# Two transformer layers on one core: other score blocks at the end of layer 1, whole score groups repeated, a later stop of the VectorE units

## The chip, the cores and the metric

The kernel runs on one core of one Trainium2 chip. The metric is the device time in microseconds (us); the time before is the median of seven runs. A separate run was profiled; its trace gives every instruction of every engine, the DMAs, and the clock that was granted to TensorE.

## The reference

Two layers of attention and a feed-forward part, with the same weights twice. Sequence 2048, width 448, 16 heads of 28, hidden width 1792, all in bf16.

```python
def _A_ref(x, wqkv, wo):
    B, S, D = x.shape
    H = 16; Dh = D // H
    qkv = (x @ wqkv).reshape(B, S, 3, H, Dh).transpose(2, 0, 3, 1, 4)
    q, k, v = qkv[0], qkv[1], qkv[2]
    scores = jnp.einsum("bhqd,bhkd->bhqk", q, k) * Dh ** -0.5
    p = _softmax(scores, axis=-1)
    o = jnp.einsum("bhqk,bhkd->bhqd", p, v)
    return o.transpose(0, 2, 1, 3).reshape(B, S, D) @ wo

def _B_ref(x, w1, b1, w2, b2):
    h = jnp.einsum("bsd,df->bsf", x, w1) + b1
    r = jnp.where(h > 0, h, 0)
    return jnp.einsum("bsf,fd->bsd", r * r, w2) + b2

for _ in range(2):
    x = x + _A_ref(_layernorm(x), A_wqkv, A_wo)
    x = x + _B_ref(_layernorm(x), B_w1, B_b1, B_w2, B_b2)
```

## The kernel before

**Who orders the work.** The kernel is written as a set of streams (Python generators) that yield operations with an engine, a planned duration, dependencies and a buffer to take. A planner (`Planner.run`) keeps a planned clock for each engine and always takes the stream whose next operation can start first, with priorities in between; the order in which it takes them is the order in which the instructions stand on the engines' queues. So a change of one number can move instructions everywhere behind the place where it first matters.

**Blocks, passes and units.** The rows (queries) of each layer are cut into blocks, listed in `blocks` (L228) as (first tile of 128 rows, tiles). A pass is one block and one group of four heads. A unit is 512 columns of scores of one head: two key tiles for a block of 256 rows (r = 2), four for one of 128 (r = 4). Each layer has 1024 units, however it is cut.

**Scores and exps.** `s_stream` (L693) takes three units at a time into one PSUM tile `sc` of 1536 columns; there are two such tiles. Its matmuls (L739) have 32 rows, one head each, so the three of one round (one value of `i`) work side by side in different quarters of the array. `e_stream` (L748) turns a group into probabilities `pt` with one exp of 1536 columns on ScalarE (L757). A group can be computed only when the exp two groups earlier has released its `sc` tile, and has to be ready when the exp just before it is over.

**Repeats.** TensorE's planned load over the last `HWIN` = 3.4 us is kept near `HOT` = 0.9 (`HOTE` = 0.8 for the last 100 units). Where it is lower, `s_stream` writes some of the group's matmuls again ahead of the group itself, up to `MORE` = 3 times; the results are the same values in the same places. The number is bounded by the planned room: until another operation could start on TensorE, and until the exp before is over. Each repeat counts 0.22 us in the plan. The loop over rounds is

```python
o.more = 0.22 * again
for i in [0] * again + list(range(4)):
    for k, (pi, kb, r, hh) in enumerate(us):
        if i >= r:
            continue
```

so a repeat is the first round of the group. A second filler, `heat` (L1079), puts matmuls of 448 columns on an identity (L1094) where the load is under `HEAT`.

**Units on VectorE.** `apart` (L661) sometimes gives a fourth unit to the group; its scores go into another PSUM bank (`mt`), and VectorE computes its exp with integer and polynomial steps (`a_first`, `a_rest`, L780 to L825), seven instructions. None is taken when fewer than `STOP` = 140 units remain.

**What follows.** `p_stream` (L830) multiplies probabilities by values into `oT` (L885); the denominators come along as a row of ones in the values. `norm_stream` (L942) divides: by a way over three small DMAs on SP's queue (`dn`, `scr`, `rec`), or, for the last block of a layer, by a matmul with `sel` (L957) and a reciprocal. `chain` (L1009) then adds the output projection to `x_sb`, normalises (`layernorm`, L422; the transposed tile is copied out of PSUM at L472 or L474), computes the hidden layer (L523, relu L1042 or L1044, square L1048), the second matrix, and adds or stores. `engs_now()` allows ScalarE as well as VectorE for a copy once no scores are left.

Of the kernel before, what the change touches and what calls it, by code (L numbers as in the profile page):

```python
# [11 lines left out]
DT = mybir.dt  # L12
AF = mybir.ActivationFunctionType
ALU = mybir.AluOpType
P = 128
H = 16
DH = 28
DHP = 32
G = 4
QB = 512  # L20
QR = 256
# [11 lines left out]
TILES = 1  # L33
DCLK = 0.2
OWN = 2
TG = 1
SUMS = 0
HALF = 320
BB = 0.85
TURNS = 1  # L40
# [30 lines left out]
LASTP = 3.2  # L71
# [1 line left out]
HOLD1 = 7  # L73
NL = 0
NLP = 3.8
STOP = 140
HSTOP = 0
CHUNK = 2
EV = 3.5
# [124 lines left out]
def kernel(  # L204
# [12 lines left out]
    nc = tc.nc  # L217
# [7 lines left out]

    q_scale = float(DH) ** -0.5 * float(np.log2(np.e)) * 2.0 ** 23

    blocks = [[(0, 2), (2, 2), (4, 2), (6, 2), (8, 2), (10, 2), (12, 2), (14, 2)], [(0, 2), (2, 2), (4, 2), (6, 2), (8, 2), (10, 2), (12, 1), (13, 1), (14, 1), (15, 1)]]  # L228

    x_view = A_x[0].rearrange("(tb p) d -> p tb d", p=P)  # L230
    out_view = out[0].rearrange("(tb p) d -> p tb d", p=P)
# [15 lines left out]
    pl = Planner()  # L247
# [131 lines left out]
    def bank(o, name):  # L379

        if o.res in R_m:
            return ps_m[R_m.index(o.res)].tile([P, 512], DT.float32, name=name, tag="m")[:, :]
        return ps_sc.tile([P, 3 * 512], DT.float32, name="sc", tag="sc")[:, 0:512]
# [18 lines left out]
    def engs_now(early=False):  # L402
        return ("ACT", "DVE") if (early and ("s", AEND) not in pl.tok) or len(s_left) == 0 else ("DVE",)
# [18 lines left out]
    def layernorm(t0, nt, deps_of, early=False, mv=None):  # L422


        if mv is None:
            mv = moments()
            for j in range(nt):
                yield stats(mv, t0, j, deps_of(j))
        ln = {}
        single = early and t0 == 0 and TILES  # L430
        rss = []
        for a, b in [(0, 1), (1, 2)] if single else [(0, nt)]:
            def rsqrt(e, a=a, b=b):
                rstd = sp.tile([P, 4], DT.float32, name="rstd")
                for j in range(a, b):
                    ln[j] = rstd[:, j:j + 1]
                ve = sp.tile([P, 4], DT.float32, name="ve")
                nc.gpsimd.tensor_tensor(out=ve[:, a:b], in0=mv[0][:, a:b, 1], in1=eps_t[:, a:b], op=ALU.add)  # L438
                nc.gpsimd.tensor_tensor(out=rstd[:, a:b], in0=ve[:, a:b], in1=mhalf[:, a:b], op=ALU.pow)  # L439
            rs = Op("POOL", 0.95 if early else 0.6, rsqrt, deps=[mv[1][b - 1]], sets=[("rs", t0 + a)] if early else ())  # L440
            rss += [rs] * (b - a)
            pl.spawn(EV, iter([rs]))
        box = {}

        def take(e):
            box["x"] = xtp.tile([P, NDC, QR], DT.bfloat16, name="xnT")
        own_xt = Op("DVE", 0.0, take, acq=R_xt)
        yield own_xt
        xnT = box["x"]
        ends = []  # L450
        todo = []
        evs = []

        def turn(p0, own, xs):
            box = {}

            def tr(e, xs=xs):
                tp = bank(t, "tp").bitcast(DT.bfloat16).rearrange("p (c q) -> p c q", c=NDC)
                box["t"] = tp
                for k, (xn, _) in enumerate(xs):  # L460
                    for dc in range(NDC):
                        nc.tensor.transpose(out=tp[:, dc, k * P:(k + 1) * P],  # L462
                                            in_=xn[:, dc * P:(dc + 1) * P], identity=ident[:, :])
            t = Op("PE", 0.07 * NDC * len(xs), tr, deps=[x[1] for x in xs],
                   acq=pools_now(early) if early else spare(1))
            yield t

            def ev(e, p0=p0, w=len(xs) * P):
                tp = box["t"]
                dst = xnT[:, :, p0 * P:p0 * P + w]  # L470
                if e == "ACT":
                    nc.scalar.copy(out=dst, in_=tp[:, :, 0:w])  # L472
                else:
                    nc.vector.tensor_copy(out=dst, in_=tp[:, :, 0:w])  # L474
            o = Op("DVE" if early else engs_now(), 0.12 + 0.3 * len(xs), ev, deps=[t], rel=t, sets=[("xT", t0 + p0)] if early else ())
            ends.append(o)
            evs.extend([o, Op("DVE", 0.0, None, deps=[t], rel=own)])

        wide = 1 if single else 2
        for p0 in range(0, nt, wide):  # L480
            js = range(p0, min(p0 + wide, nt))
            own = Op("DVE", 0.0, None, acq=R_xn)
            yield own
            xs = []
            for j in js:
                xn = xns[2 * (own.turn % 2) + j % 2]

                def norm(e, j=j, xn=xn):
                    nc.vector.tensor_scalar(out=xn[:, 0:D], in0=x_sb[:, t0 + j, :],  # L489
                                            scalar1=mv[0][:, j, 0:1], scalar2=ln[j],  # L490
                                            op0=ALU.subtract, op1=ALU.mult)
                nm = Op("DVE", 0.42, norm, deps=[rss[j]], sets=[("n", t0, j)] if early else ())
                yield nm
                xs.append((xn, nm))

            todo.append((p0, own, xs))
            if early and p0 + wide < nt:
                continue
            while todo:
                p0, own, xs = todo.pop(0)  # L500
                yield from turn(p0, own, xs)
        yield from evs
        return xnT, own_xt, ends
# [148 lines left out]
    gbuf = []  # L652
    where = {}
# [39 lines left out]
    def s_stream():  # L693
        while at[0] < len(units):
# [5 lines left out]
            def fn(e, gi=gi, us=us, js=js):  # L700
# [28 lines left out]
                    last = ("e" in gbuf[gi - 1] and gbuf[gi - 1]["e"].end) or pl.clock["ACT"] + 1.35  # L729
                    again = max(0, min(MORE, int(min(o.room, last - LAT["PE"] - o.end) / 0.22)))  # L730
                o.more = 0.22 * again
                for i in [0] * again + list(range(4)):
                    for k, (pi, kb, r, hh) in enumerate(us):
                        if i >= r:
                            continue
# [94 lines left out]
    def p_stream():  # L830


        for pi, (l, qb, g, kbs, first, last) in enumerate(passes):
# [15 lines left out]
                yield Op("-", 0.0, None, deps=[("u", pi, kb)])  # L849
                yield Op("-", 0.0, None, deps=[("e", gi) for gi, k, _ in where[pi, kb] if k < 3])  # L850
            yield from got(hold)
            if end and SUMS:
                box["so"] = Op("PE", 0.0, None, acq=pools_now)
                yield box["so"]
            while todo:
                now = [kb for kb in todo if done(kb)][:some]
                if len(now) < min(some, len(todo)):
# [11 lines left out]
                todo = [kb for kb in todo if kb not in now]  # L869
                begin, close = "t" not in box, not todo  # L870

                def fn(e, now=now, begin=begin, close=close, box=box, pi=pi, l=l, g=g, r=r, n=n, end=end):
                    if "t" not in box:
                        p_next[0] = None
                        box["t"] = bank(box["o"], "oT")
                        if "so" in box:
                            box["s"] = bank(box["so"], "den")
                    held[0] -= sum(k == 3 for kb in now for _, k, _ in where[pi, kb])
                    for kb in now:
                        for i in range(r):  # L880
                            for gi, k, hh in where[pi, kb]:
                                p, c0 = gbuf[gi]["pt"], k * 512 + i * n
                                if k == 3:
# [4 lines left out]
                                                 start=begin and kb == now[0] and i == 0,  # L888
                                                 stop=close and kb == now[-1] and i == r - 1,
                                                 tile_position=(0, DHP * hh))  # L890

                            for gi, k, hh in where[pi, kb] if end and SUMS else ():
                                p, c0 = (gbuf[gi]["pd"], i * n) if k == 3 else (gbuf[gi]["pt"], k * 512 + i * n)
                                nc.tensor.matmul(box["s"][DHP * hh:DHP * hh + DHP, 0:n],
                                                 lhsT=ones[:, :], rhs=p[:, c0:c0 + n],
                                                 start=begin and kb == now[0] and i == 0,
                                                 stop=close and kb == now[-1] and i == r - 1,
                                                 tile_position=(0, DHP * hh))
                by = [(("x" if k == 3 else "e"), gi) for kb in now for gi, k, _ in where[pi, kb]]
                o = Op("PE", 0.02 + 0.22 * len(now) * (2 if end and SUMS else 1), fn,  # L900
                       deps=[*by, *{("V", l, kb + i) for kb in now for i in range(r)}],
                       acq=None if "o" in box else pools_now(),
                       rel=[gbuf[gi][w] for w, gi in by], mode="col")
                box.setdefault("o", o)
                yield o
            res = {}
            if end and SUMS:
                pl.spawn(2, last_norm(l, qb, g, n, box, o))
                return

            def ev(e, box=box, first=first, last=last, g=g, res=res, n=n, l=l, qb=qb):
                src = box["t"][:, 0:n]
                if last:
# [10 lines left out]
            if last:  # L924
                pl.spawn(3, norm_stream(l, qb, g, res, oe))

    def last_norm(l, qb, g, n, box, o):
        def rcp(e):
            box["r"] = rp.tile([P, QR], DT.float32, name="rec")
            nc.vector.reciprocal(out=box["r"][:, 0:n], in_=box["s"][:, 0:n])  # L930
        r = Op("DVE", n * 0.0066 + 0.1, rcp, deps=[o], rel=box["so"], acq=R_rec)
        yield r

        def mul(e):
            nc.vector.tensor_tensor(out=oTn_of[l, qb][0][:, g, 0:n], in0=box["t"][:, 0:n], in1=box["r"][:, 0:n], op=ALU.mult)
        m = Op("DVE", 0.15 + n / 930, mul, deps=[r, oTn_of[l, qb][1]], rel=[box["o"], r])
        yield m
        norm_done.setdefault((l, qb), []).append(m)
        if len(norm_done[l, qb]) == G:
            pl.spawn(LASTP, chain(l, qb))  # L940

    def norm_stream(l, qb, g, res, oe):  # L942


        t0, nt = blocks[l][qb]
        n = nt * P
        box = {}
        tail = qb == len(blocks[l]) - 1 and not (l == 1 and SUMS and g < G - TG)
        if (l, qb) not in oTn_of:
            def take(e):  # L950
                oTn_of[l, qb][0] = np_.tile([P, G, QR], DT.bfloat16, name="oTn")
# [191 lines left out]
```

## Time and profile before

| | us |
|---|---|
| median of 7 runs | 925.67 |
| lowest and highest | 922.99, 926.24 |
| profiled execution | 932.32 |
| its span, first to last instruction | 930.5 |
| its granted TensorE clock (mean) | 0.974 |
| first exp begins, last one ends | 10.96, 913.55 |

In the page's rows the numbers after the bar are busy time, mean duration of one, and the idle time of the engine just before such instructions, with what ended it. The durations of one exp overlap (1642 ns each, but 888.8 us for 659). In the timeline a row merges equal instructions that follow each other: start, length, what, count, and the idle time ahead in brackets. In the windows each row is one stretch of time: its length, the busy time (and count) of each engine, then the granted clock as a share of full speed.

### The profile page before, as it was taken

The numbers are of one execution on the slowest core, as the hardware profiler recorded it, in microseconds if no ns is written. First come the engines' busy times: TensorE is split into PE (matmuls) and PEld (weight loads), VectorE is DVE, ScalarE is ACT, GpSimd is POOL, SyncE is SP. The second block draws the span as 40 slices with busy tenths as digits, with TensorE's granted clock in tenths as the row PEclk, the third lists the DMA queues.
The fourth block names the chain that finished last, engine by engine and source line by source line (L and its number), as shares of the span: only waits on it lengthen the run. The fifth ranks groups of instructions, "written<-read, shape, count | busy, mean of one in ns | idle before, by whom it ended". The sixth has DMA issues, their size and how long they took to land.

```text
span 930.5 us, 30373 instructions
## 1 busy us (share of the span) xinstructions
PE 825.4 (89%) x13553; PEld 474.9 (51%) x13553; DVE 665.7 (72%) x1387; ACT 899.4 (97%) x679; POOL 40.5 (4%) x91
## 2 busy tenths in 40 slices
PE   8999879988889898888989999889989988898888
PEld 4555545454455544554545454545454444555556
DVE  7754778778887877787867564678687788867444
ACT  6999999999999999999999999999999999999994
POOL 5100000000000000000000000000000000000000
PEclk9999989999999999999999999979899999989999
DMA  7100010000000000000000000011000000010000
GB/s 230 59 2 2 8 38 14 15 10 13 13 14 8 14 14 8 14 14 1 2 1 2 2 2 1 9 39 31 21 11 23 24 14 19 14 25 12 22 18 12
DMA packets 34624, 18.53 MB, mean 20 GB/s; under 512 B 18618, under 2 KB 34043, under 8 KB 34492
## 3 DMA queue, kind: packets, MB, share of 16 engines
q1 hardware_dynamic: 34492, 16.58, 6.3%
q8 instruction: 106, 1.74, 0.8%
q14 instruction: 26, 0.21, 0.1%
HBM read 14.26 MB, written 2.07 MB: 18 GB/s over the span
## 4 chain that ended last, share of the span: by engine, by line
ACT 64%; PE 17%; issue 16%; DVE 2%; POOL 0%; DMA 0%; ACTq 0%; DVEq 0%
ACT pt L757 64%; PE mt L523 6%; PE sc L739 5%; PE oT L885 3%; PE sc L523 1%; PE mt L1094 0%; DVE xn L489 0%; PE tp L462 0%; DMA x_sb<-in_A_x_dram 0%; DVE vh L809 0%; POOL rstd L439 0%; DVE st L416 0%; DVE x_sb L1006 0%; DVE xnT L474 0%; PE mt L739 0%
## 5 line engine op out<-in xcount | busy, mean ns | idle before, releaser
L757 ACT ACTIVATE pt<-sc 128x1536 bf16<-128x1536 f32 x659 | 888.8, 1642 | 12.3 <-PE sc L739 10.2
L739 PE MATMUL sc<-Q_sb,K_sb 32*128 32x256 bf16 (+1 forms) x6094 | 328.6, 266 | 95.9 <-ACT pt L757 90.5
L739 PEld LDWEIGHTS <-K_sb 32*128 32x128 bf16 x6324 | 166.4, 93 | 261.5 <-issue 250.2
L885 PE MATMUL oT<-pt,V_sb 128*32 128x256 bf16 (+1 forms) x4456 | 158.2, 272 | 0.2
L885 PEld LDWEIGHTS <-V_sb 128*32 128x32 bf16 x4608 | 97.6, 99 | 46.9 <-issue 41.3
L523 PE MATMUL mt<-xnT,w 128*128 128x256 bf16 (+1 forms) x960 | 117.4, 264 | 0.6 <-DVE r L1044 0.2
L809 DVE SCALAR_TENSOR_TENSOR vh<-vh,vm 128x512 f32<-128x512 f32 x142 | 97.2, 685 | 1.7
L523 PEld LDWEIGHTS <-w 128*128 128x128 bf16 x1008 | 81.0, 98 | 31.2 <-issue 21.5
L1044 DVE TENSOR_SCALAR r<-mt 128x512 bf16<-128x512 f32 (+1 forms) x107 | 72.7, 679 | 31.5 <-PE mt L523 30.6
L786 DVE TENSOR_SCALAR vi<-mt 128x512 int32<-128x512 f32 x71 | 48.9, 688 | 31.5 <-PE mt L739 26.3
L1006 DVE TENSOR_TENSOR x_sb<-x_sb,mt 128x448 bf16<-128x448 bf16 (+1 forms) x62 | 37.6, 607 | 36.8 <-PE mt L523 36.6
L523 PE MATMUL mt<-w,h 128*128 128x448 bf16 x224 | 52.8, 355 | 0.0
L919 DVE COPY oT_sb<-oT 128x256 f32<-128x256 f32 (+1 forms) x52 | 19.9, 382 | 43.6 <-PE oT L885 43.5
L809 DVE SCALAR_TENSOR_TENSOR vh<-vm 128x512 f32<-128x512 f32 x71 | 48.3, 680 | 0.0
L523 PE MATMUL mt<-w,V_sb 128*128 128x448 bf16 (+1 forms) x210 | 47.9, 353 | 0.0
L438 POOL TENSOR_TENSOR ve<-mv,eps_t 128x2 f32<-128x2 f32 (+1 forms) x35 | 8.4, 241 | 876.0 <-DVE mv L417 852.5
L416 DVE BATCH_NORM_STATS2 st<-x_sb 128x6 f32<-128x448 bf16 x64 | 39.4, 616 | 1.2 <-DMA x_sb<-in_A_x_dram 0.6
L739 PE MATMUL mt<-Q_sb,K_sb 32*128 32x256 bf16 (+1 forms) x230 | 39.4, 273 | 0.0
L545 DVE CAST K_sb<-mt 128x512 bf16<-128x512 f32 (+1 forms) x30 | 20.4, 680 | 22.2 <-PE mt L523 22.1
L523 PE MATMUL mt<-xnT,wk 128*128 128x256 bf16 x240 | 33.4, 279 | 0.6 <-DVE K_sb L919 0.4
L489 DVE TENSOR_SCALAR xn<-x_sb,mv,rstd 128x448 bf16<-128x448 bf16 x64 | 26.0, 420 | 10.7 <-POOL rstd L439 9.4
L523 PE MATMUL mt<-xnT,wq 128*128 128x256 bf16 x248 | 33.5, 274 | 0.0
(90 smaller groups left out, 658.8 us busy)
## 6 DMA issues: line engine op xcount, KB each, us to landing
rec<-scr SPq DMA_DIRECT2D x52, 128.0 KB
x_sb<-in_A_x_dram SPq DMA_DIRECT2D x8, 224.0 KB
out_dram<-x_sb SPq DMA_DIRECT2D x15, 112.0 KB
w<-in_B_w_dram SPq DMA_DIRECT2D x1, 1568.0 KB
w<-in_B_w_dram SPq DMA_DIRECT2D x1, 1344.0 KB
dn<-oT_sb SPq DMA_DIRECT2D x52, 4.0 KB
scr<-dn SPq DMA_DIRECT2D x52, 4.0 KB
rec<-scr SPq DMA_DIRECT2D x12, 64.0 KB
```

Of the source, the lines that this page charges most:

```text
L416: nc.vector.bn_stats(out=st[:, :], in_=x_sb[:, t0 + j, :])
L489: nc.vector.tensor_scalar(out=xn[:, 0:D], in0=x_sb[:, t0 + j, :], scalar1=mv[0][:, j, 0:1], scalar2=ln[j], op0=ALU.subtract, op1=ALU.mult)
L523: nc.tensor.matmul(box["t"][:, c0:c0 + n], lhsT=lhsT() if callable(lhsT) else lhsT, rhs=rhs, start=a, stop=b)
L545: nc.vector.tensor_copy(out=dst, in_=src)
L739: nc.tensor.matmul(dst[k][:, i * nt * P:(i + 1) * nt * P], lhsT=K_sb[l][rows, g, (kb + i) * P:(kb + i + 1) * P], rhs=Q_sb[rows, g, t0 * P: ...
L757: nc.scalar.activation(out=pt[:, 0:n], in_=gbuf[gi]["sc"][:, 0:n], func=AF.Exp, scale=float(np.log(2.0)) * 2.0 ** -23)
L786: nc.vector.tensor_scalar(out=box["i"][:, :], in0=src, scalar1=EXP_BIAS, scalar2=0.0, op0=ALU.add, op1=ALU.max)
L809: nc.vector.scalar_tensor_tensor(out=h[:, :], in0=src, scalar=b, in1=m, op0=ALU.add, op1=ALU.mult)
L885: nc.tensor.matmul(box["t"][DHP * hh:DHP * hh + DHP, 0:n], lhsT=V_sb[l][:, kb + i, 4 * g + hh, :], rhs=p[:, c0:c0 + n], start=begin and kb ...
L919: nc.vector.tensor_copy(out=dst, in_=src)
L1006: nc.vector.tensor_tensor(out=x_sb[:, tb, lo:hi], in0=x_sb[:, tb, lo:hi], in1=t[:, 0:hi - lo], op=ALU.add)
L1044: nc.vector.tensor_scalar(out=r[:, 0:w], in0=t[:, 0:w], scalar1=0.0, scalar2=None, op0=ALU.max)
```

## The change

Four edits, and the removal of switches that were off (`TG`, `SUMS` and the branches and the function `last_norm` that only `SUMS` reached):

- Layer 1's rows are cut into seven blocks of 256 and two of 128, where they were six and four.
- A repeat writes the whole group again, all rounds, not the first round alone. The planned cost of a repeat stays 0.22 us.
- `STOP` is 120, not 140.
- The transposed tile of a late `layernorm` is always copied by VectorE; before, ScalarE was allowed once no scores were left.

```diff
-STOP = 140
+STOP = 120
...
-    blocks = [[(0, 2), (2, 2), (4, 2), (6, 2), (8, 2), (10, 2), (12, 2), (14, 2)], [(0, 2), (2, 2), (4, 2), (6, 2), (8, 2), (10, 2), (12, 1), (13, 1), (14, 1), (15, 1)]]
+    blocks = [[(0, 2), (2, 2), (4, 2), (6, 2), (8, 2), (10, 2), (12, 2), (14, 2)], [(0, 2), (2, 2), (4, 2), (6, 2), (8, 2), (10, 2), (12, 2), (14, 1), (15, 1)]]
...
-            o = Op("DVE" if early else engs_now(), 0.12 + 0.3 * len(xs), ev, deps=[t], rel=t, sets=[("xT", t0 + p0)] if early else ())
+            o = Op("DVE", 0.12 + 0.3 * len(xs), ev, deps=[t], rel=t, sets=[("xT", t0 + p0)] if early else ())
...
-                for i in [0] * again + list(range(4)):
+                for i in list(range(4)) * (again + 1):
...
-            if end and SUMS:
-                pl.spawn(2, last_norm(l, qb, g, n, box, o))
-                return
...
-        tail = qb == len(blocks[l]) - 1 and not (l == 1 and SUMS and g < G - TG)
+        tail = qb == len(blocks[l]) - 1
```

More of the change, by code (lines that the diff above doesn't have):

```diff
@@ L35 @@
 OWN = 2
-TG = 1
-SUMS = 0
 HALF = 320
@@ L851, in p_stream @@
             yield from got(hold)
-            if end and SUMS:
-                box["so"] = Op("PE", 0.0, None, acq=pools_now)
-                yield box["so"]
             while todo:
@@ L870, in p_stream, with fn @@
                 begin, close = "t" not in box, not todo
-                def fn(e, now=now, begin=begin, close=close, box=box, pi=pi, l=l, g=g, r=r, n=n, end=end):
+                def fn(e, now=now, begin=begin, close=close, box=box, pi=pi, l=l, g=g, r=r, n=n):
                     if "t" not in box:
@@ L875, in fn @@
                         box["t"] = bank(box["o"], "oT")
-                        if "so" in box:
-                            box["s"] = bank(box["so"], "den")
                     held[0] -= sum(k == 3 for kb in now for _, k, _ in where[pi, kb])
@@ L890, in fn @@
                                                  tile_position=(0, DHP * hh))
[L892 to L898, printed above, removed]
                 by = [(("x" if k == 3 else "e"), gi) for kb in now for gi, k, _ in where[pi, kb]]
-                o = Op("PE", 0.02 + 0.22 * len(now) * (2 if end and SUMS else 1), fn,
+                o = Op("PE", 0.02 + 0.22 * len(now), fn,
                        deps=[*by, *{("V", l, kb + i) for kb in now for i in range(r)}],
@@ L906, in p_stream @@
             res = {}
-            if end and SUMS:
-                pl.spawn(2, last_norm(l, qb, g, n, box, o))
-                return
             def ev(e, box=box, first=first, last=last, g=g, res=res, n=n, l=l, qb=qb):
@@ L925, in p_stream @@
                 pl.spawn(3, norm_stream(l, qb, g, res, oe))
[L927 to L940, printed above, removed]
     def norm_stream(l, qb, g, res, oe):
```

## The prediction

> **What bounds the kernel now.** I read the page first for the engines' shares, then ScalarE's timeline for its stops, then the clock and the engines by windows laid on the 3.41 us grid in which the clock changes, and last one group of scores.
>
> ```profile
> PE 825.4 (89%) x13553; PEld 474.9 (51%) x13553; DVE 665.7 (72%) x1387; ACT 899.4 (97%) x679; POOL 40.5 (4%) x91
> PEclk9999989999999999999999999979899999989999
> L757 ACT ACTIVATE pt<-sc 128x1536 bf16<-128x1536 f32 x659 | 888.8, 1642 | 12.3 <-PE sc L739 10.2 <-PE mt L739 1.2 <-ACT pt L757 0.3
> ```
>
> ScalarE is the bound: 659 exps, 888.8 us of its 899.4. They run from 10.96 to 913.55; ahead of them lies the start and behind them a tail of 16.95 us. Inside, ScalarE stands still for 12.3 us in all. Where?
>
> ```profile
> 27.06 105.58 ACT L757 ACTIVATE pt<-sc 128x1536 bf16<-128x1536 f32 x78 [0.49 <-PE sc L739]
> 134.06 36.40 ACT L757 ACTIVATE pt<-sc 128x1536 bf16<-128x1536 f32 x27 [1.42 <-PE sc L739]
> 171.45 23.08 ACT L757 ACTIVATE pt<-sc 128x1536 bf16<-128x1536 f32 x17 [0.99 <-PE sc L739]
> 195.45 169.36 ACT L757 ACTIVATE pt<-sc 128x1536 bf16<-128x1536 f32 x126 [0.92 <-PE sc L739]
> 365.65 250.13 ACT L757 ACTIVATE pt<-sc 128x1536 bf16<-128x1536 f32 x186 [0.84 <-PE mt L739]
> ```
>
> In a few single stops, each behind TensorE's scores. From 134.06 to 861.24 the rows name 1.42, 0.99, 0.92, 0.84, 0.28, 0.38, 0.70, 0.92, 0.75, 0.33, 0.35, 0.45, 0.35, 0.52 and 0.88: 10.1 us. Between them 126 exps take 169.36, so (169.36 - 1.45) / 125 = 1.343 us each. The windows (PE, PEld, DVE, ACT, POOL busy, then the clock) say why:
>
> ```profile
> 123.57:126.98 3.41, 2.01 (x49) 1.32 (x49) 2.15 (x6) 3.41 (x4) 0.00 (x0) 1.00 0.17 46
> 126.98:133.80 6.82, 6.52 (x65) 2.75 (x64) 4.37 (x11) 5.53 (x4) 0.00 (x0) 0.50 0.14 40
> 188.42:191.83 3.41, 1.78 (x43) 1.21 (x43) 3.34 (x7) 3.41 (x4) 0.00 (x0) 1.00 0.04 6
> 191.83:195.24 3.41, 3.41 (x29) 1.75 (x28) 1.68 (x4) 2.67 (x2) 0.00 (x0) 0.50 0.05 12
> 266.93:270.34 3.41, 2.26 (x60) 1.11 (x52) 2.45 (x7) 3.41 (x4) 0.00 (x0) 1.00 0.00 0
> 270.34:273.75 3.41, 2.81 (x40) 1.79 (x39) 3.36 (x9) 3.41 (x4) 0.00 (x0) 1.00 0.02 1
> 652.63:656.04 3.41, 1.96 (x45) 1.10 (x38) 3.27 (x8) 3.41 (x4) 0.64 (x2) 1.00 0.00 0
> 656.04:662.87 6.83, 6.50 (x80) 3.16 (x80) 5.30 (x12) 5.78 (x5) 0.69 (x1) 0.50 0.08 22
> 679.94:683.35 3.41, 2.17 (x43) 1.36 (x42) 2.44 (x7) 3.41 (x4) 0.00 (x0) 1.00 0.03 4
> ```
>
> Every stop lies in, or just behind, a stretch at clock 0.50, and every such stretch follows a window in which TensorE was busy for 1.76 to 2.17 of 3.41 us. At 2.17 (679.94) and 2.26 (266.93) the clock stayed. So TensorE is slowed because it had too little to do; then it is too slow and ScalarE waits. There are ten such periods, 14 windows at 0.50, 0.72 us lost in each.
>
> **The change, part by part.** (Counts are from the order of instructions of both kernels.)
>
> *Whole score groups repeated.* The planner's choice of how many repeats a group gets (0 to 3, 546 in all before, 554 after) is the same in the first 577 of 659 groups, and so is everything else there; only what a repeat is changes, from the first round to both. A round is the three or four matmuls of one i, which run side by side.
>
> ```profile
> 150.34 0.72 PE L739 MATMUL sc<-Q_sb,K_sb 32*128 32x256 bf16 x15 [0.73 <-ACT pt L757]
> 26.62 0.40 PE L739 MATMUL sc<-Q_sb,K_sb 32*128 32x256 bf16 x6 [0.41 <-ACT pt L757]
> ```
>
> Five rounds take 0.72, two 0.40: 0.107 each, 0.109 from start to start. In the first 577 groups 513 repeats become 0.109 longer: 56 us of TensorE, put where it idles (825.4 of 930.5 busy now). What that does to the windows ahead of the slow ones: the groups in 188.42:191.83 have 9 repeats, so 1.78 + 0.98 = 2.76; in 123.57:126.98 8 (2.88), in 652.63:656.04 6 (2.61). The other four have 6 to 9. All end over the 2.17 that parts the two kinds. In the first 800 us that is 7.9 of the 10.1 us; the three periods behind (813, 833, 857) are planned anew with the same repeats and cost 2.2. I take off all 10.1 and leave one window, +0.7: where no repeat fits (266.93, 2.26) another position of the grid may still catch a low stretch. With the stops gone nothing else is late: the exps themselves, 1.343 each, are what remains.
>
> Its price is on two paths. First, a group with three repeats: scores at 150.34 + 0.72 + 0.33 = 151.39, and 0.10 to the exp that waits (as ahead of 171.45): 151.49. That exp ends at 152.98 and takes 1.45 alone, so it may start at 151.53. It fits by 0.04 us, 134 times. Bounds: nothing, or, if a round took 0.119, 0.04 each, 5.4 us; I take 0.3, since the five rounds measured show no such spread. Second, what stands behind the group on TensorE's queue (hidden layer, o, transposes, in their order) comes up to 0.33 later, then the next scores; repeats are put where the plan has no other work ready, and I leave that within the 0.3. In the start, the fifth group (three repeats) delays the key matmuls behind it: 0 to 0.33, taken as 0.2.
>
> Here the Trainium skill speaks against the change. TensorE: Matmul & The Clock Gate, section "Why this matters for your kernels", says that a window of idle drops the clock[...]. TensorE here has no gap of 3 us: it is 52 to 64% busy in the windows that are followed by 0.50. By the rule filling gaps of under a microsecond buys nothing and the sum is -0.4 us; by the rows it is -9.7. I follow the rows: ten of ten.
>
> *The blocks.* Rows 1536 to 1791 in one block of 256 rather than two of 128: 256 fewer weight loads for o, 56 fewer for the hidden layer, twelve of the small DMAs on SP's queue fewer (64 sets of three become 60), two fewer POOL instructions. None is on ScalarE, and ScalarE's units stay 2048. A later block means a longer wait before its hidden layer (57 us of exps instead of 29), but two blocks of 128, some 57 us, still follow it. Cost 0; without that cover its second 128 rows would lie in the tail, 56 hidden matmuls of 0.055 and 18 of 0.19 (rows at 921.61 and 917.90): some 6.5 us.
>
> *Units on VectorE until 120 remain.* 71 become 73, so 1977 units on ScalarE become 1975: 658 exps of three units and a last one of one unit. A 1536-wide exp alone takes 1.45, ScalarE's relu of 512 columns 0.60: -0.85 us, straight off the path. VectorE gets 2 x 4.3 us (seven instructions of 0.42 to 0.69) where it is 40% idle (65.5 of 113.6 us after 800): free, unless it makes an o copy late.
>
> *The copy of xnT on VectorE in the tail.* ScalarE's took 0.59 at 920.97 with TensorE waiting 0.67 for it; VectorE's of that form take 0.42: -0.16. But of the 56 hidden matmuls of the last block but one, 16 stand ahead of the last exp's o matmuls before, none after: +0.9 us of TensorE in the tail, mostly under the waits of the last block's normalisation (917.6 to 920.5). Bounds -0.5 and +0.9; I take +0.16, so 0 with the copy.
>
> Sum, in the profiled execution (932.32, its span 930.5): -10.1 + 0.7 - 0.85 + 0.3 + 0.2 = -9.7: 922.6.
>
> The median of seven, 925.67, lies 6.65 under the profiled run, even under its span. Two readings. Either tracing costs that much and the median run loses its 10 us too: 916.0. Or instructions run as traced and the median run has fewer slow periods: then nothing falls below 922.6. The Trainium skill (Runtime: NRT & Kernel Launch, section "The ~15µs preamble/postamble breakdown") gives a fixed 6.2 us between profile and execution, spent after the kernel. The size is right, the place is not, as the span holds it. By the second reading the fastest run (922.99) would have had one slow window where the trace has 14; I lean to the first, with 12 windows (8.6 us) in the median run: 925.67 - 8.6 + 0.7 - 0.85 + 0.5 = 917.4.
>
> **The rivals.**
>
> 1. *The slow windows go* (0.80): 914 to 923, 917.4 likeliest.
>
> 2. *They stay* (0.11), since what the clock watches is not the busy time I read, or each window filled leaves the next as low. For: the rule above; a repeat adds no finished work. Against: busy time parts the windows without an exception in those shown. Time: 925.67 - 0.4 = 925.3; with half of them gone 921.
>
> 3. *Slower* (0.09): the groups with three repeats come too late. They fit by 0.04 us. If rounds back to back take 0.122 rather than 0.109, eight rounds are 0.10 later, ScalarE waits 0.067 in each of 134 groups, 9 us, and the gain is gone; from there on it is slower, and at 0.13 it is 0.13 x 134 = 17 us lost: 925.67 - 9 + 17 = 933. For: slack so thin is nowhere used now. Against: rounds have kept to 0.109, and a group late by 0.1 is cheap unless the next one is too.
>
> **How the numbers follow.** The range, 913.5 to 924, holds the first case but for 0.03, and the half of the second with a gain; what is left out is the rest of 2 and all of 3. 0.2% (1.85 us) is what a measurement of this kernel can tell from none. Faster than 923.8: 0.82 (case 1 and a little of 2). Within: 0.09. Slower: 0.09.
>
> **What would show it.** PEclk at 9 throughout and a granted clock over 0.99 (0.974 now); ScalarE's rows running for hundreds of microseconds without a stop; idle before the exps near 3 us, not 12.3; 659 exps, the last of 512 columns. Wrong: windows at 0.50 as many as before (case 2), or the same clock with idle before the exps spread over a hundred stops behind TensorE's scores (case 3), or a tail over 18 us.

## The result, and the profile after

The changed kernel takes 923.24 us (median of 26 runs, 921.82 to 927.53), the kernel before 925.98 (61 runs beside it, 922.48 to 932.45). The ratio is 0.9969, 95% interval 0.9958 to 0.9981: faster by 0.3%, some 2.7 us, where 8.3 were forecast. The profiled execution took 921.82 (span 920.0), where 922.6 was forecast and the profiled execution of before took 932.32. So the step from one profiled execution to the next came out, and the step to the median did not.

The page of after: busy time of each engine, the granted clock by slices, and the row of the exps.

```profile
PE 860.4 (94%) x14796; PEld 515.4 (56%) x14796; DVE 672.6 (73%) x1387; ACT 895.9 (97%) x678; POOL 39.6 (4%) x89
PEclk9999999999999999999999999999999999999999
L755 ACT ACTIVATE pt<-sc 128x1536 bf16<-128x1536 f32 x659 | 885.9, 1511 | 4.5 <-PE sc L737 2.2
```

There is no slice below full clock left; the mean granted clock went from 0.974 to 1.000, and with it the idle time before the exps from 12.3 us to 4.5. TensorE is busy 35 us more.

The windows of after, laid where the exps are those of two windows that the prediction showed (123.57 and 188.42); columns as there.

```profile
125.10:128.51 3.41, 2.80 (x70) 2.01 (x66) 2.78 (x6) 3.41 (x3) 0.00 (x0) 1.00 0.14 40
187.40:190.81 3.41, 2.62 (x68) 2.05 (x68) 3.34 (x8) 3.41 (x4) 0.00 (x0) 1.00 0.04 6
```

TensorE's busy time in these stretches was 2.01 and 1.78 of 3.41 us and is now 2.80 and 2.62 (forecast: 2.88 and 2.76), over the 2.17 that parted the two kinds of window before. The two stretches are cut for this comparison and not on the grid of this execution's clock; on that grid the emptiest window, 12.04 to 15.45, has 2.29.

ScalarE's timeline of after: all runs of exps from 27 us on, and in brackets the stop ahead of each.

```profile
27.03 69.96 ACT L755 ACTIVATE pt<-sc 128x1536 bf16<-128x1536 f32 x52 [0.49 <-PE sc L737]
97.61 10.93 ACT L755 ACTIVATE pt<-sc 128x1536 bf16<-128x1536 f32 x8 [0.62 <-PE mt L737]
109.15 10.92 ACT L755 ACTIVATE pt<-sc 128x1536 bf16<-128x1536 f32 x8 [0.61 <-PE mt L737]
120.69 478.65 ACT L755 ACTIVATE pt<-sc 128x1536 bf16<-128x1536 f32 x356 [0.62 <-PE sc L737]
599.72 24.29 ACT L755 ACTIVATE pt<-sc 128x1536 bf16<-128x1536 f32 x18 [0.38 <-PE mt L737]
624.38 278.66 ACT L755 ACTIVATE pt<-sc 128x1536 bf16<-128x1536 f32 x208 [0.38 <-PE mt L737]
```

356 exps run without a stop, where the longest stretch was 186. The fifteen stops of the slow windows are gone. Five others have come: 0.62, 0.61, 0.62, 0.38 and 0.38, together 2.6 us, at full clock, and four of them are put down to `mt`, the bank of the fourth unit. The forecast had 0.3 us for late groups, spread over many, and no such stops.

### The profile page after: what moved, and what is told of

The parts are those of the page before. It is cut to its first block, busy times and chain, and to the rows that moved or that the text cites. A ratio compares the mean times of both kernels' runs of the same rounds, so it can differ in the third digit from the quotient of the medians.

```text
span 920.0 us, 32836 instructions
## 1 busy us (share of the span) xinstructions
PE 860.4 (94%) x14796; PEld 515.4 (56%) x14796; DVE 672.6 (73%) x1387; ACT 895.9 (97%) x678; POOL 39.6 (4%) x89
## 4 chain that ended last, share of the span: by engine, by line
ACT 66%; PE 20%; issue 12%; DVE 1%; DMA 0%; POOL 0%; ACTq 0%
ACT pt L755 66%; PE sc L737 7%; PE mt L521 6%; PE oT L878 4%; PE sc L521 1%; PE tp L460 1%; DVE xn L487 0%; PE mt L737 0%; DMA x_sb<-in_A_x_dram 0%; PE mt L1060 0%; POOL rstd L437 0%; DVE st L414 0%; PE den L923 0%; DVE rec L929 0%; DVE x_sb L972 0%
## 5 line engine op out<-in xcount | busy, mean ns | idle before, releaser
L737 PE MATMUL sc<-Q_sb,K_sb 32*128 32x256 bf16 (+1 forms) x7576 | 384.2, 266 | 52.1 <-ACT pt L755 49.0
L737 PEld LDWEIGHTS <-K_sb 32*128 32x128 bf16 x7882 | 215.0, 92 | 218.4 <-issue 209.5
L878 PE MATMUL oT<-pt,V_sb 128*32 128x256 bf16 (+1 forms) x4204 | 149.6, 268 | 0.7 <-DVE rec L929 0.3
L878 PEld LDWEIGHTS <-V_sb 128*32 128x32 bf16 x4352 | 92.7, 96 | 43.4 <-issue 40.9
L807 DVE SCALAR_TENSOR_TENSOR vh<-vh,vm 128x512 f32<-128x512 f32 x146 | 99.9, 684 | 1.7
L1010 DVE TENSOR_SCALAR r<-mt 128x512 bf16<-128x512 f32 x106 | 72.5, 684 | 30.3 <-PE mt L521 29.5
L521 PE MATMUL mt<-w,V_sb 128*128 128x448 bf16 (+1 forms) x224 | 50.8, 351 | 0.0
L737 PE MATMUL mt<-Q_sb,K_sb 32*128 32x256 bf16 (+1 forms) x306 | 48.9, 269 | 0.0
```

What stands on the lines that cost most here:

```text
L521: nc.tensor.matmul(box["t"][:, c0:c0 + n], lhsT=lhsT() if callable(lhsT) else lhsT, rhs=rhs, start=a, stop=b)
L737: nc.tensor.matmul(dst[k][:, i * nt * P:(i + 1) * nt * P], lhsT=K_sb[l][rows, g, (kb + i) * P:(kb + i + 1) * P], rhs=Q_sb[rows, g, t0 * P: ...
L807: nc.vector.scalar_tensor_tensor(out=h[:, :], in0=src, scalar=b, in1=m, op0=ALU.add, op1=ALU.mult)
L878: nc.tensor.matmul(box["t"][DHP * hh:DHP * hh + DHP, 0:n], lhsT=V_sb[l][:, kb + i, 4 * g + hh, :], rhs=p[:, c0:c0 + n], start=begin and kb ...
L1010: nc.vector.tensor_scalar(out=r[:, 0:w], in0=t[:, 0:w], scalar1=0.0, scalar2=None, op0=ALU.max)
```

## The experiments

In every run of every kernel the time is 1.7 to 2.2 us over the span, and its mean granted clock is on record. The traces show the clock at 1.00 or 0.50 and nothing between, so (1 - clock) x 2 x span / 3.413 is the number of windows at 0.50 in that run (14.2 for the trace of before, whose rows have 14). A line through the 57 runs of before in the two sets gives 920.4 us plus 0.78 per window (correlation 0.92, 3.2 to 14.7 windows). I use that below to tell what a kernel takes without slow windows from what the windows cost.

**The whole repeats alone.** The kernel before, with one line of the change:

```diff
-                for i in [0] * again + list(range(4)):
+                for i in list(range(4)) * (again + 1):
```

> The kernel before with one line changed: a repeat writes the whole group. Theory A (the ordinary run of before loses only about 3.8 us in slow clock windows, since its profiled run, 932.3, was one of its slowest and no run was under 922.5; the whole repeats take these away but bring 2.6 us of new stops, in five groups whose fourth unit shares a quarter of the array with another): 3.8 - 2.6 = about 1 us faster, ratio 0.998 to 1.000, clock 0.997 or more, and the five stops of 0.4 to 0.6 us before the exps in the trace. Theory B (the ordinary run loses 8.6 us as predicted, and what was gained is given back by the other edits, the blocks and the tail): 919 to 920, ratio 0.993.

Measured: 925.1 us (12 runs), before beside it 928.21 (23 runs), ratio 0.9975 (0.9958 to 0.9992). The median run has no slow window, where that of before has 9.2; the seven runs without one take 924.27. So the windows go, as the first case said, and the trace has the five stops of after (0.62, 0.61, 0.62, 0.38, 0.38). The gain of 3.1 us is more than the 1 us expected, since before lost more to windows in this set. But the kernel without windows is 3.5 us slower than the 920.8 at which before's line on that chip ends at no window. About half of what the windows gave is eaten by a price outside them.

**The change without it.** The same line the other way round, in the kernel after.

> The changed kernel with a repeat of the first round alone, as before: blocks, the stop at 120 and the copy on VectorE remain. Theory A: -0.85 (one exp of a third the length) + 0.3 (tail): 925.4, ratio 0.999 to 1.000, the clock as low and as scattered as in the kernel before (0.98 to 1.0). Theory B: the other edits give some 5 us back: 930, ratio 1.005.

Measured: 924.75 (12 runs), ratio 0.9976 (0.9948 to 1.0004), with 6.5 windows in the median run (1.1 to 11.9); its line is 919.5 plus 0.88 per window. So the slow windows are back. And the price shows again: the runs of after that have no window take 922.8 (12 runs), 3.3 above that 919.5. The two runs give the same account from both sides: whole repeats take off some 5 to 7 us of slow windows and cost some 3.4. (That is less sure than it looks: a line's end lies outside its runs, and after was not run again beside this kernel.)

**No repeats at all.** The kernel before with the same planned order, the repeats planned but not written:

```diff
-                for i in [0] * again + list(range(4)):
+                for i in range(4):
```

> The kernel before, same order of instructions, but no repeat is written at all (549 rounds of 0.109 us less on TensorE). If the clock follows TensorE's busy time as the windows show (both theories): many more windows at 0.50, granted clock 0.93 or lower, 30 or more windows at 0.7 us each: 945 us or more, ratio 1.02 or more. If it does not: TensorE has 60 us less to do and nothing else changes: 922 to 926, ratio 0.996 to 1.000, clock 0.97 or more.

Measured: 937.3 (4 runs), ratio 1.0108 (1.0068 to 1.0147). Its page:

```profile
PE 796.0 (85%) x11837; PEld 426.7 (46%) x11837; DVE 665.3 (71%) x1387; ACT 900.0 (97%) x679; POOL 40.7 (4%) x91
PEclk9999968989999999999999999968899998899999
L757 ACT ACTIVATE pt<-sc 128x1536 bf16<-128x1536 f32 x659 | 889.5, 1613 | 13.1 <-PE sc L739 11.9
```

TensorE has 1716 matmuls fewer to do and the kernel is slower: there are 34 to 41 slow windows in a run (clock 0.925 to 0.938). That is the number expected, but the time is not: at 0.7 us each it was to be 945 or more. Measured from the 920.8 of no window, each costs 0.44 us on average, and ScalarE's idle time before the exps, 13.1 us in a trace with 34 windows, is hardly more than the 12.3 of before with 14. So the cost of a window is not one number. With the first experiment this is a series in one quantity: no repeats 38 windows, first-round repeats 7 to 9, whole repeats none in the median run. The order of instructions is the same in all three, so windows do follow from too little TensorE work.

**The price: whose matmuls are late.** TensorE's rows of after ahead of the stop at 97.61, and a group with three whole repeats without a fourth unit:

```profile
95.82 0.27 PE L737 MATMUL mt<-Q_sb,K_sb 32*128 32x256 bf16 x1
96.04 0.27 PE L737 MATMUL mt<-Q_sb,K_sb 32*128 32x256 bf16 x1
96.26 0.27 PE L737 MATMUL mt<-Q_sb,K_sb 32*128 32x256 bf16 x1
...
97.35 0.27 PE L737 MATMUL mt<-Q_sb,K_sb 32*128 32x256 bf16 x1
97.61 1.45 ACT L755 ACTIVATE pt<-sc 128x1536 bf16<-128x1536 f32 x1 [0.62 <-PE mt L737]
...
596.71 1.05 PE L737 MATMUL sc<-Q_sb,K_sb 32*128 32x256 bf16 x24 [0.43 <-ACT pt L755]
```

The ordinary group keeps to the forecast: 24 matmuls, eight rounds, in 1.05 us. In the group with the fourth unit the `mt` matmuls start 0.22 apart (95.82, 96.04, 96.26), twice the 0.109 of a round; from 95.82 to 97.35, seven steps, 0.219 each. The list of units as the program is built gives the reason. Usually a group's fourth unit belongs to the head that the three leave free (heads 2, 3, 0 and then 1). In just five groups with repeats it has a head that is among the three (3, 0, 1 and then 0). There the pass is almost at its end, and `apart` takes the first unit of the next pass, which is always head 0. Then two of a round's four matmuls use the same quarter of the array. Counted from 0, these are groups 61, 69, 77, 433 and 451, and by the counts of ScalarE's rows (2 + 1 + 2 + 4 + 52 = 61, then 8, 8, 356 and 18 more) exactly their exps stand behind the five stops. Three of the five have three repeats and two have two, as there are three stops of 0.62 and two of 0.38; the 17 groups with three repeats and four different heads have no stop. Eight such rounds take 1.75 us, more than the 1.343 of the exp that should cover them. A variant of after leaves the fourth unit out of the repeats, and keeps it in the group itself:

```diff
-                for i in list(range(4)) * (again + 1):
-                    for k, (pi, kb, r, hh) in enumerate(us):
+                for i, w in [(i, 3) for i in range(4)] * again + [(i, 4) for i in range(4)]:
+                    for k, (pi, kb, r, hh) in enumerate(us[:w]):
```

> The changed kernel, but a repeat leaves the fourth unit out (the group itself has all four). Theory A: the five stops of 0.38 to 0.62 us are gone (2.6 us), the clock stays at 0.998 or more: 920.6, ratio to before 0.994. If the stops come from how late these groups start, and not from two units in one quarter of the array: 923, ratio 0.997, and the stops are still in the trace. Theory B says nothing of it: 923.

Measured: 920.69 (6 runs), ratio 0.9929 (0.9903 to 0.9955). Its ScalarE timeline from 27 us on:

```profile
27.17 602.83 ACT L755 ACTIVATE pt<-sc 128x1536 bf16<-128x1536 f32 x448 [0.49 <-PE sc L737]
630.16 4.17 ACT L755 ACTIVATE pt<-sc 128x1536 bf16<-128x1536 f32 x3 [0.17 <-PE sc L737]
634.75 266.57 ACT L755 ACTIVATE pt<-sc 128x1536 bf16<-128x1536 f32 x199 [0.41 <-PE sc L737]
```

All five stops are gone (two small ones, 0.17 and 0.41, have come), with 158 matmuls fewer; 448 exps run without a stop, and the granted clock stays at 1.000. The runs without slow windows take 920.09 here and 919.40 in the second set below, against 922.8 in after: a price of 2.7 to 3.4 us, across sets, in which the chips differ by 0.7. In the traces of the two kernels, neither with a slow window, the time from the first exp's start to the last one's end differs by 1.9 us.

**The other three edits**, each undone in this variant, with the variant itself once more in the same set. First the stop at 140 units again:

```diff
-STOP = 120
+STOP = 140
```

> As the kernel with repeats of three units, but VectorE units until 140 remain, as before. 72 instead of 73 units go to VectorE, so the last exp has 1024 columns instead of 512. If a unit counts by its exp alone: (1.45 - 0.60) / 2 = 0.43 us slower than e8 in runs without a slow window. If the later stop makes VectorE late somewhere: no slower, or faster.

then ScalarE allowed for the late copy of the transposed tile:

```diff
-            o = Op("DVE", 0.12 + 0.3 * len(xs), ev, ...
+            o = Op("DVE" if early else engs_now(), 0.12 + 0.3 * len(xs), ev, ...
```

> As the kernel with repeats of three units, but the transposed tile in the tail may be copied by ScalarE again. By the durations alone (0.59 against 0.42) 0.16 us slower than e8, and the order of the tail may go back to the one before, whose tail was 0.3 us shorter (16.7 against 17.0 us from the last exp to the end): between 0.3 us faster and 0.16 slower. The clock and the stops as in e8.

then layer 1 in six blocks of 256 and four of 128 again:

```diff
-... (10, 2), (12, 2), (14, 1), (15, 1)]]
+... (10, 2), (12, 1), (13, 1), (14, 1), (15, 1)]]
```

> As the kernel with repeats of three units, but layer 1 in six blocks of 256 and four of 128, as before. By the prediction the blocks cost and bring nothing; the last exp has 1024 columns: 0.43 us slower than e8. If the blocks are what makes the remaining difference in runs without a slow window (the edits other than the repeats brought about 1.3 us where the shorter exp and the tail explain 0.55): 1.2 us slower than e8.

and the variant as it was:

> The kernel with repeats of three units once more, as what the other three are compared with: 920 to 921, ratio 0.993 to 0.995, at most one slow window in a run.

Measured, with 34 runs of before at 926.51; the last column takes only the runs in which no window was slow, since one such window is as large as what is sought:

| | median us | ratio (95%) | without slow windows |
|---|---|---|---|
| variant as it was | 919.71 (11 runs) | 0.9933 (0.9910 to 0.9956) | 919.40 |
| stop at 140 | 920.88 (12) | 0.9948 (0.9931 to 0.9965) | 919.80 |
| old blocks | 920.4 (12) | 0.9947 (0.9930 to 0.9964) | 920.26 |
| copy on either engine | 921.56 (12) | 0.9955 (0.9933 to 0.9976) | 921.21 |

The stop at 140 costs 0.40, as expected: its last exp has 1024 columns and ends 0.92 us after the one before it, the variant's has 512 and ends 0.49 after, 0.43 less. The old blocks cost 0.86, between the two expected; their last exp has 1024 columns too, which is 0.40 of it, and 0.45 is left that no row explains; the two profiled executions, each with one slow window, are 921.92 and 921.85. The copy is a miss: 1.8 us slower, where at most 0.16 was expected. The tail of that kernel, from 905 us on (TensorE, and ScalarE's copy):

```profile
907.17 0.40 PE L460 MATMUL tp<-ident,xn 128*128 128x128 bf16 x4 [1.46 <-DVE xn L487]
...
907.61 0.59 ACT L470 COPY xnT<-tp 128x512 bf16<-128x512 bf16 x1 [1.70 <-PE tp L460]
908.54 1.95 PE L521 MATMUL sc<-xnT,w 128*128 128x128 bf16 x32
...
911.67 1.68 PE L521 MATMUL mt<-w,V_sb 128*128 128x448 bf16 x8
...
913.32 2.06 PE L521 MATMUL sc<-w,V_sb 128*128 128x320 bf16 x14
```

The same stretch of after, whose last exp ends 2.18 us later:

```profile
907.78 2.24 PE L521 MATMUL mt<-w,V_sb 128*128 128x448 bf16 x11
909.86 0.39 PE L460 MATMUL sc<-ident,xn 128*128 128x128 bf16 x4
910.08 0.73 PE L521 MATMUL mt<-w,V_sb 128*128 128x448 bf16 x3
910.28 0.42 DVE L472 COPY xnT<-sc 128x512 bf16<-128x512 bf16 x1 [0.57 <-PE sc L460]
910.76 1.07 PE L521 MATMUL mt<-xnT,w 128*128 128x128 bf16 x16
...
914.03 2.07 PE L521 MATMUL mt<-w,V_sb 128*128 128x320 bf16 x14
```

The hidden layer of the last block starts at 908.54 with ScalarE's copy and at 910.76 - 2.18 = 908.58 with VectorE's: the copy's own speed changes nothing. What changes is the planned order of the second matrix of the block before (the rows of 448 columns). In after it fills the wait for the last normalisation, 11 matmuls ahead of the transposes and 3 behind. With the copy on either engine TensorE stands idle there for 1.46 us, and eight of these matmuls (1.68 us) come behind the last hidden layer, in front of the last block's second matrix, which starts at 913.32 rather than at 914.03 - 2.18 = 911.85. The exps' end to the kernel's end is 18.97 us there and 16.95 in after.

**The best version** is the variant that leaves the fourth unit out of the repeats: 920.69 and 919.71 us in two sets on two chips, 0.7% under before, where the change as given brings 0.3%.

## Why the prediction was right and wrong

*What bounds it, and the clock: right.* The windows of 3.41 us with little TensorE work were the cause of the slow clock and of the stops. The series of no, first-round and whole repeats shows it. The Trainium skill (TensorE: Matmul & The Clock Gate, "Why this matters for your kernels") asks for no idle gaps over about 3 us between bursts; taken to mean that shorter ones are harmless, it would have made the repeats worth nothing. In before the clock fell after windows with no gap over 0.93 us. The rows decided for 9.7 us in the profiled execution, and that is where it went: no slow window in it, 10.5 us less.

*The profiled sum of -9.7: right to 0.8, with two terms wrong against each other.* The exps ran from 10.96 to 913.86 in before (913.55 in the table and the prediction is a slip of 0.31, which makes the tail of 16.95 one of 16.64) and run from 10.93 to 903.05 in after: 10.8 less. Their idle time gives 7.8 of that, 12.3 less 4.5; without the five new stops it would be 10.4. The other 2.9 is their busy time, which I had left as it was but for the last exp (0.85, see below). Every stop also ends an overlap of about 0.1 us of one exp with the next, so ten stops fewer are some 1.1 of it; the rest, about 1, was not taken apart. I had allowed 0.7 for a window that stays; this execution has none. So the 2.3 too little for the late groups was more than made up by the 2.1 of busy time and this 0.7, and that the sum came so near was in part luck.

*"Groups late, 0.3": the first step that failed.* It measured 2.6 us in the trace's stops, and 2.7 to 3.4 from the runs without slow windows. I argued over a slack of 0.04 us in 134 groups with a round of 0.109; 131 of them have no stop, and the three that have one do not keep that round. I had taken "the three or four matmuls of one i, which run side by side" for all groups. For a fourth unit of a head already in the group it is wrong, and the trace of before showed it, in TensorE's rows of the same group:

```profile
95.85 0.27 PE L739 MATMUL mt<-Q_sb,K_sb 32*128 32x256 bf16 x1
96.07 0.27 PE L739 MATMUL mt<-Q_sb,K_sb 32*128 32x256 bf16 x1
96.29 0.27 PE L739 MATMUL mt<-Q_sb,K_sb 32*128 32x256 bf16 x1
```

0.22 apart there too: with first-round repeats five rounds, 1.1 us, which an exp covers; with whole repeats eight, 1.75, which it does not. The third rival had the right kind of loss in the wrong groups: five late by 0.4 to 0.6 (two of them with two repeats), not 134 by 0.07. (Its sum comes to 933.7, not 933.)

*From the profiled execution to the median: the second step that failed.* I read the 6.65 us between them as the cost of tracing and put 12 slow windows, 8.6 us, into the median run. The line of the runs gives 931.5 for 14.2 windows, so at most 0.8 of the 932.32 is left for tracing, within the scatter of the runs about the line; and in the sets above profiled executions stand anywhere from fastest to slowest. The second reading was the right one: the number of slow windows differs from run to run of one program, and the profiled execution, with 14, was at the upper end of 3 to 15. The median run of before has (925.98 - 920.4) / 0.78 = 7, worth 5.6 us by that line. With 3.0 us too much here and 2.3 too little for the late groups, 5.3 of the 5.6 us by which -8.3 missed -2.7 are accounted for. I had set that reading aside because it left the fastest run with one slow window where the trace has 14; by the line it has about 3, and that is within what runs of one program do.

*The window left, 0.7: right.* The median run of after has 0.8 such windows, and lies 0.7 over the end of its own line at no window. *The last exp, -0.85: right.* Exps overlap, so what one adds is read from end to end: the last one of after ends at 902.11 + 0.94 = 903.05, the one before it at 902.56, so it adds 0.49, where every full exp adds 1.34. The stop at 140 agrees for the smaller step that it makes. *The start, 0.2:* nothing; the row of exps at 27.06 begins at 27.03. *The blocks, 0:* 0.45 faster in the one run of them, cause open. *The copy and the tail, 0:* the sum held (16.95 against 16.64), but its parts did not. With the edit undone the tail is 2.0 longer, by an order that I had not planned through.

## What to carry to other kernels

Where a clock that follows the load costs time, count the slow windows of every run, not of the profiled one alone: here the profiled execution lost twice what the median run loses, and such a filler cannot gain more than the median run has to lose. A filler that is cheap on average is priced on the groups of another shape: look in the trace of before for the instructions that it will repeat, by kind, and compare each kind with its cover. An edit to one copy in a planned tail is weighed with the planned order that it brings, which here was worth 1.8 us where the two copies differ by 0.17.

## What the runs showed of the hardware

- Two matmuls of 32 rows in the same quarter of the array, within a round of four, took 0.219 us a round rather than 0.109, at full clock.
- The number of windows at clock 0.50 varied from 3.2 to 14.7 between runs of one program whose order is fixed. The traces show one way in which it can: the grid of 3.41 us lies elsewhere in every execution. Counted from the span's start, its first whole window begins at 0.68 us in before, at 1.80 in after and at 2.89 in the first experiment. The variant was traced twice, and the grid cut its start in two ways (columns as in the windows above; the second set first, then the first set):

```profile
13.61:17.02 3.41, 1.92 (x30) 1.03 (x29) 3.41 (x6) 2.42 (x4) 2.35 (x2) 1.00 0.34 99
17.02:20.43 3.41, 3.41 (x44) 1.75 (x37) 2.53 (x7) 2.59 (x2) 1.00 (x3) 0.50 0.95 296
...
12.13:15.54 3.41, 2.35 (x19) 1.06 (x16) 3.10 (x4) 3.35 (x4) 3.27 (x5) 1.00 0.08 18
15.54:18.95 3.41, 2.98 (x57) 1.91 (x58) 3.34 (x10) 2.48 (x3) 0.24 (x1) 1.00 0.88 229
```

In the second set a window with 1.92 us of TensorE is followed by one at 0.50. In the first set the same work (1.92 us from 13.36 to 16.77) falls into windows of 2.35 and 2.98, and the clock stays. That this explains all of the 3.2 to 14.7 is not shown.

- Busy time parts the windows well, but not without exception: without whole repeats one with 1.89 us (633.81:637.22) kept the clock, and without repeats one with 2.20 (626.56:629.97) lost it.
- What a slow window costs depends on the kernel and the place: 0.44 us on average without repeats (its four runs alone rise by 0.9 per window), 0.78 in before, 0.88 in the change without whole repeats, 1.3 in after (a line through its 26 runs, which have at most 3.3 windows each). In the variant's second trace the one window is in the start and costs 1.5 (the row of exps from 27.17 begins at 28.90, with the first exp 0.25 later). The trace of whole repeats alone has two in the start, 3.0 together, and two from 828.92 on, with stops of 0.51, 0.82, 0.43 and 0.92. A fuller TensorE losing more at half the clock would explain the order; where the windows of the runs without a kept trace lie is not known.
